# Thirty quarters of zeros: from fifteen plain writes on SyncE's queue to three casting writes on GpSimd's

## The chip, the core and the metric

The kernel runs on one core of a Trainium2 chip. The metric is the device time of one execution in microseconds (us). Each kernel is run several times and the median is given; one execution is also profiled.

The engines in play: TensorE (PE, matmuls; PEld is its weight load), VectorE (DVE), ScalarE (ACT), GpSimd (POOL), SyncE (SP, which here only issues DMAs), and 16 DMA engines which serve all queues. A queue is named by who issues into it; in the profile q1 is SyncE's, q10 ScalarE's, q0 GpSimd's, and q8 and q14 load instructions.

## What is computed

The inputs are `x` and `f_logit` (4 x 5056 x 256, four-byte floats), a gate vector, and the weights of eight experts (256 x 1024 and 1024 x 256 each). A recurrence runs along the 5056 steps of each of the 4 sequences, and each of the 20224 tokens that come out is sent to the expert with the largest logit. An expert keeps only the 80 tokens with the largest gate weight. All other rows of the output are zero.

```python
for t in range(S):
    h = f[:, t] * h + i[:, t] * x[:, t]      # f, i from a sigmoid of f_logit
    y[:, t] = h
# y as (20224, 256)
out = np.zeros((N, D), dtype=np.float32)
for e in range(E):
    tok_idx = np.where(expert_idx == e)[0]
    if len(tok_idx) > capacity:              # capacity = 80
        keep = np.argpartition(-gate_w[tok_idx], capacity)[:capacity]
        tok_idx = tok_idx[keep]
    h = np.maximum(x[tok_idx] @ w1[e], 0.0)
    out[tok_idx] = gate_w[tok_idx, None] * (h @ w2[e])
```

So 20.7 MB of zeros are written, and at most 640 rows of 1 KB are written over them.

## The kernel before

**Stage one, to about 120 us.** `f_logit` and `x` come in as 40 units (10 groups of 512 steps by 4 sequences; the last group is shorter), 512 KB each for either input. For each unit ScalarE makes the sigmoid, GpSimd the product, TensorE turns both to channels, VectorE runs the recurrence into `h_all`, TensorE makes the logits. SyncE issues all loads of this stage but one.

**Zeros.** The output is cut into 79 *quarters* of 256 rows (256 KB). The first four are written from a small zeroed tile (`first_zeros`). The list `zeros` holds the other 75 by number; two helpers take them from its front. `clear(k, m)` (L183) copies m quarters from the first four, so from output to output, with no buffer in SBUF. `wipe(m)` (L532 to L539) writes m pairs of quarters from `bare`, a weight buffer that ScalarE has filled with zeros (L530); 128 partitions of 4 KB make 512 KB, so a `wipe` of one is two quarters.

**Weights.** The experts' weights are 32 pieces of 512 KB, numbered here from 0 in the order in which TensorE uses them (`order`). They go round through a ring of 7 buffers that the first stage has set free (`ring`). `bare` lies in the last of them, which is the buffer of weight 6. A loop (L542) issues weights 0 to 6, with zeros after each: `m` counts of `wipe`, `k` quarters of `clear`. The tile framework puts in the waits: weight 6 is loaded only when every reader of `bare` is done with it, wherever in the program that reader stands. The other weights are issued by `more(1)` when TensorE has used up a buffer; the 11 quarters that are then left go between them.

**Order of work.** The schedule is written by hand (`tc.manual_schedule()`): each engine issues its instructions in the order of the program text, and an instruction that waits holds up those behind it on its own engine. SyncE issues every weight and every zero.

**Stage two, about 124 to 146 us.** The largest candidates are ranked. GpSimd fills `wide` with zeros (L666), then makes `level` (L667, L669) from `vals`, and `what` (L670, L678). VectorE makes `taken` from `level` (L687) and at last `trow`, the addresses of the chosen tokens. From about 146 us VectorE, ScalarE and GpSimd gather the chosen columns of `h_all` (L781), and from 149.7 us TensorE works through the experts: `hidden` (L817) with the first weights, `result` (L836, L846) with the second. The rows are scattered into the output (L873), after all zeros are in place.

Of the kernel before, what the change touches and what calls it, by code (L numbers as in the profile page):

```python
# [10 lines left out]
BF16 = mybir.dt.bfloat16  # L11
# [7 lines left out]
P = 128  # L19
# [16 lines left out]
def kernel(  # L36
# [11 lines left out]
    nc = tc.nc  # L48
    B, S, D = x.shape
    E, _, F = w1.shape  # L50
# [114 lines left out]
    ZR = 8  # L165
    ZC = 512
    ZQ = 4
    QP = P // ZQ
# [4 lines left out]
    zeros = list(range(ZQ, N // (QP * ZR)))  # L173
# [11 lines left out]
    def clear_some(m):  # L185
        while m > 0 and zeros:
            k = zeros[0]
            n = min(m, ZQ - k % ZQ, len(zeros))
            clear(k, n)
            del zeros[:n]  # L190
            m -= n
# [310 lines left out]
    for pool in ld[:-1]:  # L502
# [4 lines left out]
    order = sorted(((which, e, i) for which in (1, 2) for e in range(E) for i in range(2)),  # L507
                   key=e_step)
    order[-4], order[-3] = order[-3], order[-4]
    RING = 7  # L510
# [3 lines left out]
    def weights(which, e, i):  # L514
        t = ring[order.index((which, e, i)) % RING].tile([P, F], F32, name="w_sb", tag="w_sb")
        if which == 1:
            nc.sync.dma_start(out=t, in_=w1[e][ds(i * P, P)])
        else:
            t = t.rearrange("p (c d) -> p c d", c=CH)
            parts = 2 if (which, e, i) == order[-1] else 1  # L520
            n = CH // RUN // parts
            for k in range(parts):
                nc.sync.dma_start(
                    out=t.rearrange("p (h j) d -> p h j d", j=RUN)[:, ds(k * n, n)],
                    in_=w2[e][ds(i * FH + k * FH // parts, FH // parts)].rearrange(
                        "(h p j) d -> p h j d", p=P, j=RUN))
        return t

    bare = spare.tile([P, F], F32, name="w_sb", tag="w_sb")
    nc.scalar.activation(bare, ones.broadcast_to([P, F]), ACT.Copy, scale=0.0)  # L530
    BR = F // D

    def wipe(m):
        for _ in range(m):
            k = zeros[0]
            assert zeros[1] == k + 1 and 2 * QP * ZR == P * BR
            nc.sync.dma_start(out=out[ds(k * QP * ZR, P * BR)].rearrange("(p j) d -> p (j d)", p=P),
                              in_=bare)
            del zeros[:2]  # L539

    w_sb = {}
    for key, m, k in zip(order[:RING], (0, 0, 0, 0, 0, 15, 0), (0, 0, 2, 2, 1, 7, 7)):  # L542
        w_sb[key] = weights(*key)
        wipe(m)
        clear_some(k)
# [86 lines left out]
    with tc.tile_pool(name="sel", bufs=1) as sel:  # L632
# [27 lines left out]
        for k in range(BY_DVE, DEEP):  # L660
# [3 lines left out]
        what = sel.tile([P, DEEP, 2, E], F32, name="what")  # L664
        level = sel.tile([P, DEEP], F32, name="level")
        nc.gpsimd.memset(wide, 0.0)  # L666
        nc.gpsimd.tensor_scalar(out=level, in0=vals, scalar1=NONE, scalar2=-GONE,  # L667
                                op0=ALU.is_le, op1=ALU.mult)
        nc.gpsimd.tensor_tensor(level, level, bar, ALU.add)  # L669
# [281 lines left out]
    with tc.If(unsure > 0):  # L951
        with tc.tile_pool(name="all", bufs=1) as sel, \
# [34 lines left out]
            for g in range(NJ):  # L987
                nc.gpsimd.indirect_dma_start(
                    out=tok[:, ds(g, 1)], out_offset=None, in_=id_list,
# [46 lines left out]
```

## Time and profile before

| | us |
|---|---|
| median of 3 runs | 209.92 (209.12 to 211.46) |
| the profiled execution | 210.38 |
| its span in the profile | 208.6 |
| TensorE busy | 179.1 (86%) |
| VectorE busy | 152.1 (73%) |
| ScalarE busy | 137.7 (66%) |
| GpSimd busy | 131.5 (63%) |

80.10 MB pass through the 16 DMA engines at a mean of 384 GB/s. The span runs from the first to the last instruction of the profiled execution; 1.8 us of its time lie around it. Times in the rows below are counted from the span's start. The page cuts the span into 40 equal slices and gives for each the busy share of an engine in tenths (9 is 90% or more). A row of a wait names who waited, for whom, the total, how often, and the longest; the one named is the last that came.

### The profile page before, as it was taken

How to read it: one execution, taken by the hardware profiler on the slowest of the kernel's cores; microseconds unless marked ns; L12 is line 12 of the kernel's file. 1: busy time of each engine (PE TensorE's matmuls, PEld its weight loads, DVE VectorE, ACT ScalarE, POOL GpSimd, SP SyncE). 2: the span in 40 equal slices, each digit the busy share in tenths (PEclk: the TensorE clock that was granted, in tenths of full speed). 3: DMA queues.
4: the chain of work that ended last, by engine and by line, in shares of the span. 5: the costliest groups of instructions: out<-in, count | busy, mean ns of one | idle time of the engine just before them, and what ended most of it. 6: DMA issues, size and time to landing. Idle time of an engine off the chain costs nothing. (4 is left out here: it accounts for less than half of the span.)

```text
span 208.6 us, 7058 instructions
## 1 busy us (share of the span) xinstructions
PE 179.1 (86%) x2599; PEld 154.6 (74%) x2599; DVE 152.1 (73%) x485; ACT 137.7 (66%) x425; POOL 131.5 (63%) x245
## 2 busy tenths in 40 slices
PE   7779679999989999999989939798876899999880
PEld 7566568787878787887877817797875799987760
DVE  5587668999998989998999994894767637560020
ACT  2878498889887878787988952170994652771020
POOL 3385787989898878988697757100997540500621
PEclk9999999999999999999999976799999988999995
DMA  5999999999999999999999899999898999999941
GB/s 215 409 398 414 418 421 434 401 417 422 415 420 417 413 421 394 409 401 405 420 384 454 328 427 402 418 419 451 330 430 332 416 409 352 333 402 413 404 155 38
DMA packets 22541, 80.10 MB, mean 384 GB/s; under 512 B 2994, under 2 KB 2996, under 8 KB 21972
## 3 DMA queue, kind: packets, MB, share of 16 engines
q1 hardware_dynamic: 22112, 78.40, 94.3%
q0 software_dynamic: 240, 0.66, 0.9%
q8 instruction: 22, 0.36, 0.7%
q10 hardware_dynamic: 148, 0.53, 0.6%
q14 instruction: 19, 0.16, 0.2%
HBM read 70.00 MB, written 21.36 MB: 438 GB/s over the span
## 5 line engine op out<-in xcount | busy, mean ns | idle before, releaser
L278 POOL TENSOR_TENSOR x_t<-f_t,x_t 128x1024 f32<-128x1024 f32 (+1 forms) x39 | 91.2, 2346 | 16.5 <-DMA x_t<-in_x_dram 9.6
L327 DVE TENSOR_TENSOR_SCAN h_all<-h_all,up 128x512 f32<-128x512 f32 x72 | 86.1, 1254 | 5.8 <-ACT h_all L312 4.8
L312 ACT ACTIVATE h_all<-sp,nomlb 128x512 f32<-128x512 f32 x72 | 45.5, 682 | 10.0 <-PE sp L292 10.0
L274 ACT ACTIVATE f_t<-f_t 128x1024 f32<-128x1024 f32 (+1 forms) x40 | 42.1, 1053 | 10.6 <-DMA f_t<-in_f_logit_dram 9.7
L292 PE MATMUL up<-ident,x_t 128*128 128x128 f32 x288 | 38.0, 275 | 5.4 <-POOL x_t L278 5.2
L292 PE MATMUL sp<-ident,f_t 128*128 128x128 f32 x288 | 39.3, 279 | 0.7 <-ACT f_t L274 0.7
L292 PEld LDWEIGHTS up<-ident,x_t 128*128 128x128 f32 x288 | 31.9, 140 | 8.2 <-POOL x_t L278 7.8
L292 PEld LDWEIGHTS sp<-ident,f_t 128*128 128x128 f32 x288 | 30.9, 140 | 7.8 <-issue 5.2
L781 POOL COPY xe<-h_all 128x8 uint8 x160 | 22.2, 200 | 18.6 <-DVE xt L788 11.7
L339 PE MATMUL lg<-h_all,wg 128*32 128x128 f32 (+1 forms) x640 | 27.4, 286 | 6.3 <-ACT ls L348 4.0
L781 DVE COPY xe<-h_all 128x8 uint8 x256 | 20.5, 163 | 10.9 <-issue 10.8
L781 ACT COPY xe<-h_all 128x8 uint8 x224 | 22.7, 194 | 4.4 <-issue 2.8
L339 PEld LDWEIGHTS lg<-h_all,wg 128*32 128x32 f32 x640 | 15.4, 109 | 13.7 <-ACT ls L348 6.1
L817 PE MATMUL h_ps<-xt,w_sb 128*64 128x80 f32 x512 | 22.1, 240 | 2.9 <-DVE xt L788 1.9
L817 PEld LDWEIGHTS h_ps<-xt,w_sb 128*64 128x64 f32 x512 | 19.8, 142 | 4.0 <-DVE xt L788 2.1
L836 PE MATMUL y_ps<-hid,w_sb 128*64 128x80 f32 x448 | 19.2, 238 | 3.8 <-issue 1.7
L836 PEld LDWEIGHTS y_ps<-hid,w_sb 128*64 128x64 f32 x448 | 17.2, 140 | 5.5 <-issue 4.0
L197 PE MATMUL warm<-ident 128*128 128x128 f32 x128 | 19.4, 321 | 1.4 <-POOL ident masks.py:199 1.4
L197 PEld LDWEIGHTS warm<-ident 128*128 128x128 f32 x128 | 18.7, 234 | 1.6 <-POOL ident masks.py:199 1.4
L873 POOL DMA_INDIRECT out_dram<-y,goal x5 | 5.1, 1022 | 18.9 <-DMA w_sb<-in_moe_w_dram 14.2
L826 ACT ACTIVATE hid<-h_ps 128x320 f32<-128x320 f32 x16 | 6.5, 432 | 9.0 <-PE h_ps L817 8.9
L870 DVE TENSOR_SCALAR y<-y_ps,gsl 128x256 f32<-128x256 f32 x4 | 1.9, 480 | 12.9 <-DMA out_dram<-y,goal 11.1
(142 smaller groups left out, 143.9 us busy)
## 6 DMA issues: line engine op xcount, KB each, us to landing
f_t<-in_f_logit_dram SPq DMA_DIRECT2D x36, 512.0 KB, 6.3
x_t<-in_x_dram SPq DMA_DIRECT2D x35, 512.0 KB, 6.7
w_sb<-in_moe_w_dram SPq DMA_DIRECT2D x31, 512.0 KB, 8.3
out_dram<-w_sb SPq DMA_DIRECT2D x15, 512.0 KB, 10.0
out_dram<-out_dram SPq DMA_DIRECT2D x27, 256.0 KB, 7.5
f_t<-in_f_logit_dram SPq DMA_DIRECT2D x4, 448.0 KB, 5.1
x_t<-in_x_dram SPq DMA_DIRECT2D x4, 448.0 KB, 5.8
out_dram<-out_dram SPq DMA_DIRECT2D x2, 768.0 KB, 8.4
```

The costliest lines, as they stand in the source:

```text
L197: nc.tensor.matmul(warm, ident, ident, start=True, stop=True)
L274: nc.scalar.activation(s_t, s_t, ACT.Sigmoid, scale=-1.0)
L278: (nc.gpsimd if n else nc.vector).tensor_tensor(u_t, sts[n], u_t, ALU.mult)
L292: nc.tensor.transpose(at, t[:, ds(r * D + o * P, P)], ident)
L312: nc.scalar.activation(columns(n, o).rearrange("c (p r) -> c p r", r=R), sps.pop((n, o)).rearrange("c (r p) -> c p r", r=R), ACT.Identity, ...
L327: nc.vector.tensor_tensor_scan(h, h, ups.pop((n, o)), last, ALU.mult, ALU.add)
L339: nc.tensor.matmul(lgs[g][ds(r * LC, LC), b, :k], wg[:, o], h[:, r], start=o == 0, stop=o == DC - 1, skip_group_check=True)
L781: copy(xe[:, :, ds(WORD * (k + j), WORD)], pair(v - HOME))
L817: nc.tensor.matmul(HP[e, i][ds(j, HC), c], w[1, e, o][:, at:at + (HC - 1) * RUN + 1:RUN], XT[e][:, o], start=o == 0 and c == 0, stop=o == ...
L826: nc.scalar.activation(HID[e, i], HP.pop((e, i)), ACT.Relu)
L836: nc.tensor.matmul(YP[e][ds(j, HC), o], w[2, e, i][:, c, ds(o * P + j, HC)], HID[e, i][:, c], start=i == 0 and c == 0 and o == 0, stop=i = ...
L873: one = nc.gpsimd.indirect_dma_start(out=out, out_offset=bass.IndirectOffsetOnAxis(ap=goal[:, ds(g, 1)], axis=0), in_=Y.pop(g), in_offset= ...
```

## The change

SyncE's fifteen `wipe` writes are dropped (the count 15 becomes 0). In their place a new helper, `widen(n, m)`, issues n transfers on GpSimd's queue, each of m blocks of 512 KB, taken from the front of `zeros`; `widen(3, 5)` is three transfers of 2.5 MB (as written), 30 quarters in all. It reads `bare` as two-byte floats, 1024 of them in each partition, m times over, and writes four-byte floats, 20 KB in one piece for each partition. The call stands in GpSimd's program behind the fill of `wide` and ahead of `level`. The `clear` counts stay, so the numbers of the quarters that each helper takes shift; 11 quarters are left for the spread between the later weights, as before.

```diff
+    def widen(n, m):
+        k = zeros[0]
+        assert zeros[2 * n * m - 1] == k + 2 * n * m - 1 and 2 * QP * ZR == P * BR
+        small = bare.bitcast(BF16)[:, :F].unsqueeze(1).broadcast_to([P, m, F])
+        for _ in range(n):
+            nc.gpsimd.dma_start(
+                out=out[ds(zeros[0] * QP * ZR, m * P * BR)].rearrange(
+                    "(p m j) d -> p m (j d)", p=P, m=m), in_=small)
+            del zeros[:2 * m]
+
     w_sb = {}
-    for key, m, k in zip(order[:RING], (0, 0, 0, 0, 0, 15, 0), (0, 0, 2, 2, 1, 7, 7)):
+    for key, m, k in zip(order[:RING], (0, 0, 0, 0, 0, 0, 0), (0, 0, 2, 2, 1, 7, 7)):
         w_sb[key] = weights(*key)
         wipe(m)
         clear_some(k)
...
         nc.gpsimd.memset(wide, 0.0)
+        widen(3, 5)
         nc.gpsimd.tensor_scalar(out=level, in0=vals, scalar1=NONE, scalar2=-GONE,
                                 op0=ALU.is_le, op1=ALU.mult)
```

## Rows read from the trace of the kernel before

**Rows 1.** The page's head, and the busy shares in 40 slices (tenths).

```profile
span 208.6 us, 7058 instructions
PE 179.1 (86%) x2599; PEld 154.6 (74%) x2599; DVE 152.1 (73%) x485; ACT 137.7 (66%) x425; POOL 131.5 (63%) x245
...
DMA  5999999999999999999999899999898999999941
```

**Rows 2.** The DMA queues: packets, MB, share of 16 engines' span.

```profile
q1 hardware_dynamic: 22112, 78.40, 94.3%
q0 software_dynamic: 240, 0.66, 0.9%
q8 instruction: 22, 0.36, 0.7%
```

**Rows 3.** Stretches: us, then each engine's busy time, PEclk, DMA share, GB/s.

```profile
30.00:100.00 70.00, 67.16 (x834) 56.92 (x833) 65.56 (x76) 58.89 (x82) 61.32 (x31) 1.00 1.02 413
130.00:146.00 16.00, 13.62 (x110) 13.10 (x110) 11.69 (x41) 5.62 (x23) 1.23 (x5) 0.89 1.05 429
146.00:150.00 4.00, 3.41 (x35) 3.22 (x35) 3.02 (x36) 4.00 (x42) 3.92 (x28) 1.00 0.96 396
150.00:152.00 2.00, 2.00 (x64) 2.00 (x60) 1.60 (x22) 2.00 (x22) 2.00 (x15) 1.00 0.61 168
...
173.00:183.00 10.00, 10.00 (x268) 9.62 (x266) 6.54 (x73) 5.76 (x43) 2.74 (x20) 0.98 0.97 341
```

**Rows 4.** Timeline of SyncE's queue: start, us, issue, count.

```profile
121.05 0.39 SPq L523 DMA_DIRECT2D w_sb<-in_moe_w_dram  x1
122.52 15.62 SPq L537 DMA_DIRECT2D out_dram<-w_sb  x15
139.05 3.00 SPq L183 DMA_DIRECT2D out_dram<-out_dram  x3
149.50 0.35 SPq L517 DMA_DIRECT2D w_sb<-in_moe_w_dram  x1
...
151.11 0.56 SPq L523 DMA_DIRECT2D w_sb<-in_moe_w_dram  x1
```

**Rows 5.** Waits of SyncE's queue, 120 to 152 us: total, times, longest.

```profile
SPq L517 <- DMA out_dram<-w_sb: 7.3, 1, 7.3
```

**Rows 6.** Timeline of TensorE: start, us, group, count, idle before it and its releaser.

```profile
159.83 0.36 PE L836 MATMUL y_ps<-hid,w_sb 128*64 128x80 f32 x4 [1.71 <-issue]
...
161.94 1.33 PE L836 MATMUL y_ps<-hid,w_sb 128*64 128x80 f32 x32 [0.65 <-DMA w_sb<-in_moe_w_dram]
...
165.18 1.52 PE L836 MATMUL y_ps<-hid,w_sb 128*64 128x80 f32 x32 [0.75 <-DMA w_sb<-in_moe_w_dram]
```

**Rows 7.** Waits of TensorE from 149 to 206 us.

```profile
PE y_ps L836 <- issue: 1.7, 1, 1.7
PE y_ps L836 <- DMA w_sb<-in_moe_w_dram: 1.4, 2, 0.8
PE h_ps L817 <- DMA w_sb<-in_moe_w_dram: 0.6, 1, 0.6
PE y_ps L836 <- SPq L951: 0.5, 1, 0.5
```

**Rows 8.** Timeline of GpSimd, and of VectorE's first use of `level`.

```profile
129.70 0.34 POOL L666 MEMSET wide<- 16x304 f32 x1
134.79 0.32 POOL L667 TENSOR_SCALAR level<-vals 128x12 f32<-128x12 f32 x1 [4.75 <-ACT last_of L640]
...
140.93 0.17 DVE L687 SCALAR_TENSOR_TENSOR taken<-rank,level 128x12 f32<-128x12 f32 x1
```

**Rows 9.** GpSimd's scatter: duration in ns, and us from issue to landing.

```profile
L873 POOL DMA_INDIRECT out_dram<-y,goal x5: 974/976/1202, 194.2 to 203.1; - x5
...
DMA to landing us min/median/max: 2.4/4.5/5.7
```

**Rows 10.** DMA issues of the weights: count, KB each, median us to landing.

```profile
w_sb<-in_moe_w_dram SPq DMA_DIRECT2D x31, 512.0 KB, 8.3
```

## The prediction

> **What bounds the kernel now.** I read first the head of the page, its slices and its queues. The 16 DMA engines stand at nine tenths or more in nearly every slice up to the last two, while the busiest compute engine, TensorE, has 86% [rows 1]. Almost all of that is one queue, SyncE's: 78.40 MB in 94.3% of the engines' time [rows 2]. The table by stretches then says what a byte costs. From 30 to 100 us the core only loads (HBM to SBUF) and takes back a few output-to-output copies: 413 GB/s at a share of 1.02, that is 405 at a share of one. From 130 to 146 us the 15 writes out of the zeroed buffer run (SBUF to HBM): 429 at 1.05, that is 409. From 146 to 150 us come mostly copies from output to output, which touch no SBUF: 396 at 0.96, that is 412 [rows 3]. (A packet counts where it starts, so a share can pass 1.) On each route a byte costs the same: the engine is what is full, not a side of it. One stretch of 2 us has a hole: 0.61 of the engines at 150 to 152 us. Another, 173 to 183 us, runs at 341 GB/s, where weights are asked for only as TensorE frees their buffers.
>
> Then SyncE's own order. It issues weight 5 at 121.05, the 15 zero writes from 122.52 to 138.14, seven quarters of copies at 139.05, and weight 6 at 149.50 [rows 4]. The 7.3 us ahead of weight 6 are a wait for the last zero write [rows 5]: weight 6 goes into the buffer that the zeros are read from. The seven copies, issued before that wait, feed the engines meanwhile, so the wait costs only the hole. Last, TensorE: it first runs short of weights at 161.94 (weight 7, issued at 151.11) [rows 4, 6]. After 149 us its waits for weights make 1.4 + 0.6 us, and 0.5 us more go to the queue that asks for one [rows 7]. So TensorE and the transfers are almost level from 160 us to the end, and whatever delays weight 7 delays the end; whatever speeds the transfers up wins little more than those 2.5 us.
>
> **The change part by part.** *Removed from SyncE:* 15 issues. They pace SyncE, but the engines are full behind them, so the removal by itself is worth nothing.
>
> *Added to GpSimd:* three transfers behind the fill of `wide`, which ends at 129.70 + 0.34 = 130.04 [rows 8]. Each has 128 x 5 rows of 4 KB written and 2 KB read. GpSimd makes their descriptors itself. Before shows that only for the scatter, 976 ns for 128 rows [rows 9]. Bounds for one transfer of 640 rows: 1.0 us (as one scatter) to 5 x 0.976 = 4.9 us. Three take 3 to 14.6 us. GpSimd's next work needs `vals` and runs at 134.79; VectorE takes `level` at 140.93 [rows 8]. GpSimd has about 1.2 us of its own to do in between, so the cover is 140.93 - 130.04 - 1.2 = 9.7 us. I take 2 us each, 6 in all (a plain pattern, nearer to the one scatter's fixed cost than to five of them), which is hidden. At the upper bound the ranking would come 14.6 - 9.7 = 4.9 us late.
>
> *Same bytes written:* 15 x 524,288 = 7.86 MB, at 420 GB/s 18.7 us of all engines. What a casting transfer costs, no row shows, since before every transfer reads as much as it writes. Bounds: half (only the read bytes count), 9.4 us; the dearest queue per byte, q8, whose 0.36 MB took 0.7% of the engines where q1 pays 94.3 / 78.40 = 1.20% for a MB, is 1.94 / 1.20 = 1.6 times as dear, 30 us [rows 2]. GpSimd's own queue, q0, pays 0.9 / 0.66 = 1.36%, 1.13 times, 21.2 us [rows 2]. I take 1.0 for the casting writes: q0's row is of five small scatters with their ends counted, and the engine must still put out 4 KB for each row.
>
> *Moved without a line in the diff:* the order around weight 6. It still waits for the zeros to be read, but the seven copies that followed the zeros now go ahead of them. SyncE issues them right behind weight 5 and then stops at weight 6 with the next seven copies, weight 7 and all later ones queued behind. Seven quarters are 1.84 MB, 4.4 us at 420 GB/s. In front of the zeros instead of behind, they put off the end of the zeros and so weight 6: 149.50 + 4.4 = 153.9 us (**+4.4**).
>
> *The way back:* in before weight 7 reached TensorE 161.94 - 149.50 = 12.4 us after weight 6 was issued, partly behind the rest of the seven copies. In after the engines stand empty then. Two weights and seven quarters are 2.88 MB, 7.0 us at 413 GB/s; to this comes the latency, between 2.1 us (the quickest scatter landed after 2.4 us [rows 9], of which its 128 KB are 0.3) and twice that. So 9.1 to 11.2 us, against 12.4: -1.2 to -3.3, I take **-2.2**.
>
> *A hole ahead of the zeros:* weight 5 lands about 8.3 us after its issue [rows 10], near 129.4, and the seven copies end some 4.4 us later less the latency, near 132. GpSimd starts at 130.04. With 1 us of descriptors and 1 us of latency there is no hole; with 4.9 there are about 3.3 us more than the copies cover. I take **+1.0**.
>
> Sum: 4.4 - 2.2 + 1.0 = **+3.2 us** for weight 7, hence for TensorE at 161.94. From there on it runs with next to no wait for weights up to 191 us, so it carries the delay to the end. Bounds: 4.4 - 3.3 + 0 = +1.1, and 4.4 - 1.2 + 3.3 = +6.5.
>
> The profiled execution took 210.38 us (span 208.6 and 1.8 around it), 0.46 above the median of 209.92. It would become 213.6; against the median, 213.1.
>
> **Rivals.** *A cheap cast (faster).* If an engine's time follows the bytes it reads, the zeros take 9.4 us, weight 6 is issued near 144.5, weight 7 at 151.11 without a queue, and both arrive before they are needed. The gain ends where TensorE is level: its waits of 2.5 us, at most with the 1.7 us of its own issue stall [rows 7] as instruction loads find free engines. That gives 209.92 - 2.5 = 207.4, down to 205.7; break-even is where the zeros cost (18.7 - 3.2) / 18.7 = 0.83 of a plain write. For it speaks only that half the bytes are read; against it that the three routes of [rows 3], with and without SBUF, cost the same, as if the engine's own path set the pace and 4 KB must still leave it. The Trainium skill (DMA: Bandwidth & Descriptors, "Where 436 GB/s comes from") names the 16 ports into SBUF, 32 bytes each at 850 MHz, as the bottleneck; by that rule two-byte reads would halve the zeros, to about 9 us as an estimate from that page. The trace does not agree as far as it goes: the copies that use no SBUF port ran at the same 412 GB/s.
>
> *A dear cast.* At q8's 1.6 the zeros take 11.3 us more and nothing else is in the queues, so weight 6 waits it all out: 213.1 + 11.3 = 224.4. At q0's 1.13 it is 215.5. For it: the conversion is work that no plain transfer has.
>
> *A late GpSimd.* At the upper bound of its descriptors the ranking comes 4.9 us late, and with it the gather. TensorE has 1.7 + 0.65 us of waits [rows 6] before 161.94 to absorb it, so 2.5 us remain, in the shadow of weight 7's +3.2; with the hole at 3.3 also due then, the end is at +6.5 at most: 216.4.
>
> *A wash.* A cast at 0.75 to 0.93 of a write, or the order costing only its lower bound, +1.1: 208.5 to 212.0. Here too belongs that the transfers run on a queue of their own and change only who issues. The Trainium skill (DMA: Bandwidth & Descriptors, "Issuing engines are not separate DMA queues") says that DMAs from all three issuers share the same 16 engines, and by that alone nothing would be won or lost.
>
> **How the numbers follow.** My forecast, plain cost and the order's delay, with the late GpSimd in it: 0.50, own range 211.0 to 216.4, some 0.07 of it within 1%. Dear cast from 1.25 times up: 0.15, from 217.5. Cheap cast: 0.25, of which 0.02 stays within 1%. Wash: 0.10. A measurement of this kernel tells about 1%, 2.1 us, from no change. So faster 0.23, same 0.19, slower 0.58. The range from 206.0 to 218.5 leaves out the lower end of the cheap case (some 0.07) and most of the dear one (0.12).
>
> **What would show it.** In after: weight 6 issued near 154 and TensorE waiting for weights around 160 to 165 us, with a hole in the DMA share before 155 us, shows the order's delay. The share of q0 against its 8.5 MB gives the price of a cast: 1.2% per MB is plain, 0.6 cheap. GpSimd's three issues and the start of `level` show the cover. I am wrong if q0's share is near half, if weight 6 goes out before 149 us, or if the first gather starts late.

## The result, and the profile after

| | before, us | after, us |
|---|---|---|
| median of 19 runs each | 211.46 (209.12 to 213.81) | 212.99 (211.39 to 216.26) |
| the profiled execution | 210.38 | 211.39 |
| its span | 208.6 | 209.6 |

The ratio of after to before is 1.0105, with a 95% interval of 1.0072 to 1.0137. Of 211.46 us that is 2.2 us more (1.5 to 2.9). So the kernel became about 1% slower. (The ratio leaves out the executions in the chip's slower state, so it is not that of the two medians, which lie 1.5 us apart.) Single executions of either kernel scatter by 4 to 5 us, so the pair of profiles (1.0 us apart) can show the mechanism but not its size.

The page's head, its DMA slices in tenths, and the queues (packets, MB, share of the 16 engines' span) of after:

```profile
span 209.6 us, 7048 instructions
...
DMA  6999999999999999999999999999795999999941
...
q1 hardware_dynamic: 19952, 70.53, 84.1%
q0 software_dynamic: 2208, 8.52, 12.1%
```

7.86 MB moved from SyncE's queue to GpSimd's, and two slices fall to 7 and 5 tenths where [rows 1] has 8 and 8. The timeline of SyncE's queue (start, us, issue) shows what happened at its left edge, and the wait row of the same queue (total, times, longest) names the cause:

```profile
119.61 0.39 SPq L523 DMA_DIRECT2D w_sb<-in_moe_w_dram  x1
120.79 1.16 SPq L183 DMA_DIRECT2D out_dram<-out_dram  x2
152.42 0.33 SPq L517 DMA_DIRECT2D w_sb<-in_moe_w_dram  x1
152.79 1.77 SPq L183 DMA_DIRECT2D out_dram<-out_dram  x3
154.66 0.53 SPq L523 DMA_DIRECT2D w_sb<-in_moe_w_dram  x1
...
SPq L517 <- DMA out_dram<-w_sb: 30.3, 1, 30.3
```

Weight 5 at 119.61, the seven copies right behind it, and then SyncE stands for 30.3 us until the zeros have been read out of weight 6's buffer. In before it stood 7.3 us at the same place, with the zeros and the seven copies issued in between [rows 4, 5]. Weight 7 goes out at 154.66, against 151.11.

The stretches show that the transfers ran dry while SyncE stood. The columns are those of [rows 3]; the last three are PEclk, DMA share and GB/s. First before:

```profile
131.00:149.00 18.00, 16.47 (x135) 16.06 (x135) 13.23 (x69) 7.84 (x51) 4.11 (x25) 0.91 1.06 435
149.00:153.00 4.00, 2.59 (x66) 2.28 (x64) 3.02 (x34) 4.00 (x42) 4.00 (x29) 1.00 1.03 369
```

The same stretches of after, and the next:

```profile
131.00:149.00 18.00, 15.51 (x146) 14.78 (x147) 13.36 (x73) 8.99 (x62) 6.14 (x35) 1.00 1.23 415
149.00:153.00 4.00, 2.86 (x84) 2.70 (x81) 2.62 (x31) 4.00 (x43) 4.00 (x30) 1.00 0.27 85
153.00:157.00 4.00, 3.93 (x114) 3.77 (x110) 2.92 (x33) 4.00 (x34) 3.76 (x28) 1.00 1.41 461
```

From 149 to 153 us only 85 GB/s move. At 415 that stretch would have carried (415 - 85) x 4 = 1.32 MB more, which is 3.2 us of transfers lost. Before had its hole here too [rows 3], but a small one. (A packet counts where it starts, and the copies' packets are long, so the 461 behind the hole is partly work that runs on after 157.)

TensorE then pays for it. Its timeline in after (start, us, group, count, idle before it and releaser), its longest waits from 149 to 206 us, and one stretch of 1 us:

```profile
156.95 1.28 PE L828 MATMUL h_ps<-xt,w_sb 128*64 128x80 f32 x32
163.73 2.40 PE L847 MATMUL y_ps<-hid,w_sb 128*64 128x80 f32 x32 [5.51 <-DMA w_sb<-in_moe_w_dram]
165.89 1.59 PE L828 MATMUL h_ps<-xt,w_sb 128*64 128x80 f32 x32
...
203.42 0.60 PE L952 MATMUL h_ps<-ident,yc 128*128 128x128 f32 x2
...
PE y_ps L847 <- DMA w_sb<-in_moe_w_dram: 5.5, 1, 5.5
PE h_ps L828 <- DVE xt L799: 1.1, 1, 1.1
...
164.00:165.00 1.00, 1.00 (x20) 1.00 (x19) 0.86 (x12) 0.00 (x0) 0.00 (x0) 0.50 0.88 340
```

It waits 5.51 us for weight 7, where before waited 0.65 [rows 6], and starts on it at 163.73 instead of 161.94. After the idle time the granted clock is 0.50 from 164 to 165 us, the lower of the two levels (1.2 GHz), and 32 matmuls take 2.40 us instead of 1.33 [rows 6]. Behind that nothing waits long for a weight again, and the last group ends at 204.02: the delay is carried to the end.

GpSimd's side, from its timeline and from the view of the line that issues the zeros (duration in ns, first and last start; then us to landing):

```profile
129.17 2.69 POOL L546 DMA_DIRECT2D out_dram<-w_sb  x3
133.99 0.30 POOL L678 TENSOR_SCALAR level<-vals 128x12 f32<-128x12 f32 x1 [2.12 <-ACT last_of L650]
...
L546 POOL DMA_DIRECT2D out_dram<-w_sb x3: 910/920/1088, 129.2 to 130.8; - x3
...
DMA to landing us min/median/max: 10.8/16.0/21.5
```

Each issue takes 0.9 us, the three are over at 131.86, and GpSimd then idles 2.12 us for ScalarE, as it idled 4.75 us before [rows 8]. The last transfer lands 21.5 us after its issue at 130.8, that is at 152.3, just ahead of weight 6.

### The profile page after: what moved, and what is told of

It is laid out like the page before. It is cut to its first block, busy times and chain, and to the rows that moved or that the text cites. A ratio compares the mean times of both kernels' runs of the same rounds, so it can differ in the third digit from the quotient of the medians.

```text
span 209.6 us, 7048 instructions
## 1 busy us (share of the span) xinstructions
PE 176.5 (84%) x2599; PEld 152.9 (73%) x2599; DVE 150.6 (72%) x485; ACT 137.9 (66%) x425; POOL 134.0 (64%) x248
## 3 DMA queue, kind: packets, MB, share of 16 engines
q0 software_dynamic: 2208, 8.52, 12.1%
## 5 line engine op out<-in xcount | busy, mean ns | idle before, releaser
L847 PE MATMUL y_ps<-hid,w_sb 128*64 128x80 f32 x448 | 19.7, 242 | 7.0 <-DMA w_sb<-in_moe_w_dram 5.5
L828 PE MATMUL h_ps<-xt,w_sb 128*64 128x80 f32 x512 | 21.6, 236 | 2.8 <-DVE xt L799 1.6
L847 PEld LDWEIGHTS y_ps<-hid,w_sb 128*64 128x64 f32 x448 | 17.7, 143 | 8.3 <-issue 8.0
L197 PE MATMUL warm<-ident 128*128 128x128 f32 x128 | 17.9, 304 | 1.4 <-POOL ident masks.py:199 1.4
L197 PEld LDWEIGHTS warm<-ident 128*128 128x128 f32 x128 | 17.3, 218 | 1.6 <-POOL ident masks.py:199 1.4
L881 DVE TENSOR_SCALAR y<-y_ps,gsl 128x256 f32<-128x256 f32 x4 | 1.9, 479 | 13.0 <-DMA out_dram<-y,goal 11.3
```

The lines of the kernel that those rows point to most:

```text
L197: nc.tensor.matmul(warm, ident, ident, start=True, stop=True)
L828: nc.tensor.matmul(HP[e, i][ds(j, HC), c], w[1, e, o][:, at:at + (HC - 1) * RUN + 1:RUN], XT[e][:, o], start=o == 0 and c == 0, stop=o == ...
L847: nc.tensor.matmul(YP[e][ds(j, HC), o], w[2, e, i][:, c, ds(o * P + j, HC)], HID[e, i][:, c], start=i == 0 and c == 0 and o == 0, stop=i = ...
```

## The experiments

Two theories went in. **Order:** the loss comes from seven copies standing ahead of the zeros instead of behind them, which leaves the engines empty while SyncE waits for weight 6's buffer. **Price:** the loss comes from the casting transfers being dearer than plain ones. Each ratio below is to the kernel before, measured on the same chip.

| run | ratio | 95% interval |
|---|---|---|
| after, twice more (e8_after, e9_after) | 1.0110, 1.0102 | 1.0055 to 1.0166, 1.0055 to 1.0149 |
| e1_plain, again as e9_plain | 1.0190, 1.0128 | 1.0105 to 1.0274, 1.0038 to 1.0219 |
| e2_order | 1.0060 | 1.0002 to 1.0117 |
| e5_both, again as e9_both | 0.9997, 1.0023 | 0.9951 to 1.0043, 0.9971 to 1.0076 |
| e4_behind | 1.0228 | 1.0152 to 1.0305 |
| e3_own | 1.0388 | 1.0313 to 1.0463 |
| e6_pad | 1.0015 | 0.9963 to 1.0067 |
| e7_more | 1.0044 | 0.9996 to 1.0092 |
| e9_both_plain | 1.0136 | 1.0054 to 1.0218 |

**The same transfers without the cast.** After, with four-byte zeros read:

```diff
-        small = bare.bitcast(BF16)[:, :F].unsqueeze(1).broadcast_to([P, m, F])
+        small = bare.unsqueeze(1).broadcast_to([P, m, F])
```

> The three transfers stay on GpSimd's queue and in their place, but read four-byte zeros, so nothing is cast. Theory of the order (the loss comes from weight 6 being issued later, with empty engines behind the zeros, and a cast costs what a plain write costs): as the changed kernel, +1.5 to +2.5 us over the kernel before, weight 6 near 152 to 154 us, the hole behind the zeros still there. Theory of the price (the cast is dearer: GpSimd's queue paid 12.1% for 8.52 MB, 1.42% a MB, against 84.1 / 70.53 = 1.19 on SyncE's, so 1.19 times, 3.6 us on 18.7): back at the time of before or within 0.5 us of it, weight 6 some 3 us earlier, and 1.2% a MB.

Queue, stretch, and weight 6's issue of this kernel; then, from 135 to 147 us, when next to nothing but the zeros is under way, the rows of after, of this kernel and of e2_order (below, plain zeros on SyncE's queue):

```profile
q0 software_dynamic: 2208, 8.52, 10.2%
...
131.00:149.00 18.00, 16.45 (x135) 15.88 (x134) 11.46 (x51) 6.26 (x35) 3.43 (x16) 0.91 1.01 404
...
151.71 0.33 SPq L517 DMA_DIRECT2D w_sb<-in_moe_w_dram  x1
...
135.00:147.00 12.00, 10.91 (x104) 10.53 (x103) 8.41 (x50) 6.55 (x40) 2.44 (x16) 1.00 1.25 424
135.00:147.00 12.00, 11.16 (x105) 10.78 (x104) 6.62 (x27) 4.30 (x17) 0.35 (x1) 1.00 1.03 420
135.00:147.00 12.00, 11.09 (x104) 10.71 (x104) 7.75 (x41) 5.25 (x27) 1.33 (x9) 1.00 1.03 416
```

Without the cast GpSimd's queue takes 10.2 / 8.52 = 1.20% of the engines per MB, with it 12.1 / 8.52 = 1.42%. Yet the stretch moves 404 GB/s without and 415 with it, and in the 12 us of zeros alone the rates are level: 424 with the cast, 420 without it, 416 without it on SyncE's queue. The cast's packets last longer and overlap more (the share is 1.03 here, 1.25 in after), but the throughput is that of plain ones, and weight 6 goes out only 0.7 us earlier. The total is not lower than after's. Price falls.

**The order alone, on SyncE, without the cast.** Before, with the copies ahead of the wipes:

```diff
         w_sb[key] = weights(*key)
-        wipe(m)
         clear_some(k)
+        wipe(m)
```

> The kernel before with one pair of lines swapped: the seven quarters of copies are issued ahead of the fifteen plain zero writes instead of behind them. No cast, nothing on GpSimd. Theory of the order: slower than before by 1.5 to 3 us, weight 6 issued near 153 to 154 us, a hole in the DMA share behind the last zero, TensorE's long wait for weight 7. Theory of the price, and a theory that GpSimd's issues are what costs: no difference from before, within 0.5 us.

```profile
120.03 0.38 SPq L523 DMA_DIRECT2D w_sb<-in_moe_w_dram  x1
152.12 0.34 SPq L517 DMA_DIRECT2D w_sb<-in_moe_w_dram  x1
...
149.00:153.00 4.00, 2.44 (x64) 2.28 (x64) 3.17 (x37) 3.94 (x40) 4.00 (x30) 1.00 0.26 101
...
164.69 2.31 PE L836 MATMUL y_ps<-hid,w_sb 128*64 128x80 f32 x32 [4.94 <-DMA w_sb<-in_moe_w_dram]
```

The whole signature of after is here with nothing on GpSimd and nothing cast: weight 6 at 152.12, 101 GB/s in the same 4 us, 4.94 us of waiting for weight 7, and the slow 32 matmuls behind it. So two swapped lines make the mechanism. The ratio, 1.0060, is 1.3 us (0.0 to 2.5), a little under the 1.5 to 3 expected and somewhat below after's; the intervals overlap. Part of the difference shows in the profiles: from weight 5's issue to weight 6's it is 152.12 - 120.03 = 32.09 us here and 32.81 in after. That fits with after's engines running short once more, ahead of the zeros. From 129 to 134 us, after and then e2_order:

```profile
129.00:134.00 5.00, 2.91 (x23) 2.51 (x22) 4.04 (x13) 1.28 (x5) 2.87 (x5) 1.00 0.88 284
129.00:134.00 5.00, 3.43 (x17) 3.20 (x17) 3.92 (x12) 1.25 (x5) 0.29 (x2) 0.67 0.85 350
```

That is (350 - 284) x 5 = 0.33 MB, or 0.8 us of transfers. Whether the rest of the difference is more than scatter stays open.

**Bridging the hole.** After, with seven copies given to GpSimd's queue behind the zeros. In the first kernel those are the seven that stood ahead of the zeros, in the second the seven that stand between weights 6 and 7:

```diff
-    for key, m, k in zip(order[:RING], (0, 0, 0, 0, 0, 0, 0), (0, 0, 2, 2, 1, 7, 7)):
+    for key, m, k in zip(order[:RING], (0, 0, 0, 0, 0, 0, 0), (0, 0, 2, 2, 1, 0, 7)):   # e4_behind
+    for key, m, k in zip(order[:RING], (0, 0, 0, 0, 0, 0, 0), (0, 0, 2, 2, 1, 7, 0)):   # e5_both
...
         widen(3, 5)
+        clear_some(7, nc.gpsimd)
```

> The changed kernel with the first seven quarters of copies moved from SyncE's queue to GpSimd's, behind the three casting transfers, so that they again run while weight 6 waits for the zeros, as in before. Theory of the order: the loss is gone, within 1 us of before, weight 6 near 149 to 150 us, the hole behind the zeros about as small as before; some of it may stay if the engines run empty at 128 to 131 us, since the copies no longer bridge the time until GpSimd issues (up to +3 us). Theory of the price: 3 us or more slower than before.

> The changed kernel with the second seven quarters of copies moved from SyncE's queue, where they stand behind weight 6, to GpSimd's, behind the three casting transfers. The first seven stay ahead, on SyncE's queue. So copies bridge both places where the engines ran empty: 127 to 131 us, before GpSimd's first zeros, and 149 to 153 us, while weight 6 waits for the last of them. Theory of the order (all of the loss is engines standing idle): the engines stay full, and the loss of 1% is gone: -0.5 to +0.5% against before, weight 7 about 3 us sooner behind weight 6. Theory of the price (a cast on GpSimd's queue costs more than a plain write): still about 1% slower, with no hole left to blame.

The first, e4_behind:

```profile
127.00:131.00 4.00, 2.76 (x12) 1.84 (x10) 2.74 (x9) 1.22 (x4) 3.92 (x9) 0.50 0.07 28
...
165.00 2.40 PE L848 MATMUL y_ps<-hid,w_sb 128*64 128x80 f32 x32 [5.91 <-DMA w_sb<-in_moe_w_dram]
```

It was expected to lose the loss, or to keep up to 3 us of it if the engines ran empty ahead of the zeros; it was slower still, by 4.8 us (3.2 to 6.5), which is not all accounted for. The seven copies had covered the time until GpSimd's zeros flow; without them 127 to 131 us run at 28 GB/s. The zeros end only 0.8 us earlier for that (weight 6 at 151.65), and weight 7 again has seven copies ahead of it. The hole moved; it did not close.

The second, e5_both, and its repetition's PE row:

```profile
149.00:153.00 4.00, 2.85 (x84) 2.69 (x80) 2.72 (x32) 4.00 (x42) 4.00 (x30) 1.00 1.26 497
...
159.68 1.93 PE L829 MATMUL h_ps<-xt,w_sb 128*64 128x80 f32 x32 [2.46 <-DMA w_sb<-in_moe_w_dram]
```

```profile
158.92 1.33 PE L829 MATMUL h_ps<-xt,w_sb 128*64 128x80 f32 x32 [1.54 <-DMA w_sb<-in_moe_w_dram]
```

> The third corner: the changed kernel with the second seven quarters of copies on GpSimd's queue behind the zeros. Theory of the order: as the kernel before, within 0.5%.

Here weight 6 goes out no earlier than in after (153.34), but the hole carries the seven copies, and weight 7 follows weight 6 directly. TensorE waits 2.46 us (1.54 in the repetition) for weight 6 and next to nothing for weight 7. The loss is gone, twice: 0.9997 and 1.0023. As this kernel keeps the cast and GpSimd's issues, those two cost nothing that can be measured.

**Weight 6 free of the zeros.** After, with the zeros read from a small tile of their own, 2 KB a row in e3_own (in a pool beside the others) and 512 bytes a row in e6_pad (in constants that the kernel holds anyway, so rows of 1 KB are written):

```diff
-        small = bare.bitcast(BF16)[:, :F].unsqueeze(1).broadcast_to([P, m, F])
+        small = nil.bitcast(BF16).unsqueeze(1).broadcast_to([P, m, F])              # e3_own
+        small = nil.bitcast(BF16).unsqueeze(1).broadcast_to([P, 4 * m, 2 * PAD])    # e6_pad
```

> The changed kernel, but the two-byte zeros are read from a 2 KB tile of their own that GpSimd fills at 130 us, so weight 6 no longer waits for the zeros. Casts, queue and place are as in the changed kernel. Theory of the order: the loss is gone, and as weights 6 and 7 no longer stand behind the zeros TensorE's waits of 1.4 us at 162 and 165 us go too: 0 to 2.5 us faster than before, weight 6 issued near 124 us, no hole at 150. Theory of the price: the zeros still take 3.6 us more of all engines, so still 1.5 us or more slower than before.

> The changed kernel, but the two-byte zeros are read from a 512-byte tile of their own that no later tile reuses (256 of them a row, 1 KB written a row, four times as many rows), so weight 6 waits for no zeros and no expert tile does either. Casts, queue and place as in the changed kernel. Theory of the order: weight 6 issued near 123 us, no hole near 150, and weights 6 and 7 no longer behind the zeros: 0 to 1.2% faster than before. Theory of the price: still about 1% slower. Either way, should GpSimd take over 9.7 us for the descriptors of 7680 rows (640 took 0.92 us), its ranking work and the first gather come late, by up to 2 us.

```profile
122.74 0.50 SPq L517 DMA_DIRECT2D w_sb<-in_moe_w_dram  x1
...
158.79 5.09 PE L830 MATMUL h_ps<-xt,w_sb 128*64 128x80 f32 x96 [10.32 <-DVE xt L801]
...
  DMA out_dram<-nil: 10.2, 1
...
122.42 0.98 SPq L517 DMA_DIRECT2D w_sb<-in_moe_w_dram  x1
```

In e3_own (the first three rows; the third is VectorE's wait before it writes `xt`) weight 6 goes out at 122.74 as meant, but the new tile's memory is used again by the experts' input `xt`, so the gather waits for the zeros instead and the first matmul starts at 158.79. The 3.9% are that new wait's, an artefact of the edit. e6_pad (the last row: weight 6 at 122.42) has no such neighbour: its loss is gone (1.0015), but it gains nothing measurable over before, where 0 to 1.2% was expected.

**All fourteen copies ahead of weight 6, in before.** It asks whether before's own small hole is worth closing:

```diff
-    for key, m, k in zip(order[:RING], (0, 0, 0, 0, 0, 15, 0), (0, 0, 2, 2, 1, 7, 7)):
+    for key, m, k in zip(order[:RING], (0, 0, 0, 0, 0, 15, 0), (0, 0, 2, 2, 1, 14, 0)):
```

> The kernel before with all fourteen quarters of copies between the zeros and weight 6, where before has seven ahead of weight 6 and seven behind it. No cast, nothing on GpSimd. Theory of the order: weight 6 is still issued near 149.5 us, but 8.7 us of copies then cover its wait, so before's own hole of 0.6 us at 150 to 152 us closes, and weight 7 comes right behind weight 6: 0 to 1 us faster than before. A rival (the hole in before costs nothing, since TensorE is level there): no difference.

```profile
147.67 0.35 SPq L517 DMA_DIRECT2D w_sb<-in_moe_w_dram  x1
...
160.66 1.70 PE L817 MATMUL h_ps<-xt,w_sb 128*64 128x80 f32 x32 [3.16 <-DMA w_sb<-in_moe_w_dram]
```

A miss: 0 to 1 us faster was expected, 0.9 us slower came (-0.1 to 1.9), which the rival, no difference, would also allow. Fourteen copies ahead of weight 6 keep the engines full, but it has to queue behind them, and TensorE waits 3.16 us for it.

**The square: hole or bridge, cast or plain.** That e1_plain was not faster asked for one more look. After and e1_plain were run again together with e5_both (as e9_after, e9_plain and e9_both) and with e5_both without the cast (e9_both_plain). After had been repeated once before, beside e5_both, e6_pad and e7_more (e8_after).

```diff
-        small = bare.bitcast(BF16)[:, :F].unsqueeze(1).broadcast_to([P, m, F])
+        small = bare.unsqueeze(1).broadcast_to([P, m, F])
```

> The changed kernel itself once more, unaltered, on the chip of the three below, to compare them with it. Theory of the order and theory of the price alike: 0.7 to 1.4% slower than before, weight 6 near 152 us, engines idle from about 149 to 153 us.

> The changed kernel, unaltered, as one corner of a square of four on one chip: casting or plain reads, with copies behind the zeros or without. Theory of the order: 0.6 to 1.6% slower than before, as both times until now.

> The second corner: as the changed kernel, but the zeros are read as four-byte floats, so nothing is cast. Theory of the order (the cast neither costs nor saves): within 0.5% of the changed kernel in the same call. A new theory, from the first trial of this edit (1.9% slower, and its first loads of token addresses took 3.8 us instead of 1.1 to 1.3): four-byte reads of SBUF hold those loads up, the cast spares them, so 0.7 to 1% slower than the changed kernel and the long loads again.

> The fourth corner: as the third, with four-byte reads and no cast. Theory of the order: as the third and as the kernel before, within 0.5%. The new theory of the four-byte reads: 0.7 to 1% slower than the third, with first loads of token addresses near 3.8 us.

| | hole left | hole bridged |
|---|---|---|
| two bytes read (cast) | 1.0102 | 1.0023 |
| four bytes read (plain) | 1.0128 | 1.0136 |

Bridging takes the loss away only with the cast. The profile shows where the plain kernel loses instead. GpSimd's loads of the token addresses into registers, ahead of the gather (min/median/max in ns, first and last start), in after, e9_both, e1_plain, e9_plain, e9_both_plain and e2_order in turn, then in before and e7_more:

```profile
L776 POOLq TENSOR_LOAD <-trow x16: 321/690/1300, 143.3 to 179.8; - x16
L777 POOLq TENSOR_LOAD <-trow x16: 319/689/1291, 143.6 to 177.0; - x16
L776 POOLq TENSOR_LOAD <-trow x16: 319/1024/3788, 143.5 to 179.5; - x16
L776 POOLq TENSOR_LOAD <-trow x16: 319/1012/3728, 143.5 to 181.2; - x16
L777 POOLq TENSOR_LOAD <-trow x16: 318/825/2342, 143.4 to 179.7; - x16
L765 POOLq TENSOR_LOAD <-trow x16: 318/752/2329, 143.5 to 181.1; - x16
L765 POOLq TENSOR_LOAD <-trow x16: 321/688/1452, 144.3 to 177.9; - x16
L765 POOLq TENSOR_LOAD <-trow x16: 317/691/1290, 143.4 to 178.4; - x16
```

And TensorE's wait for the gathered input in e1_plain and in e9_both_plain:

```profile
PE h_ps L828 <- DVE xt L799: 4.0, 1, 4.0
...
PE h_ps L829 <- DVE xt L800: 3.3, 1, 3.3
```

The slowest load takes 1.3 us in the two kernels that cast and 2.3 to 3.8 us in the next four, which do not, with the zeros on GpSimd's queue or on SyncE's (e2_order). In the three of them on GpSimd's queue TensorE then waits 3.3 to 4.0 us for the first input; after's longest such wait is 1.1. With the hole left, that wait hides in the one for weights (2.2 us in e1_plain, 5.5 in after); with the hole bridged nothing hides it. The two intervals of the bridged column in this comparison still overlap a little (1.0054 to 1.0218, 0.9971 to 1.0076), that of e5_both lies clear (up to 1.0043).

That the loads are held up by the plain reads themselves is not shown, and the last two rows speak against it in so simple a form. Before and e7_more read four-byte zeros too, and the last of these had not landed when their loads began at 144.3 and 143.4 us, since weight 6, which waits for it, goes out at 149.50 and 147.67. Yet their slowest loads took 1.45 and 1.29 us. In the four slow kernels weight 6 goes out later, at 151.71 to 154.06. So slow loads were seen only beside plain reads, but not beside all of them, and what makes the difference stays open.

## Why the prediction was right, and where it was off

The forecast was 213.1 us, 3.2 above a median of 209.92; measured are a median of 212.99 and, by the ratio, 2.2 us (1.5 to 2.9) more than before, whose median more runs put at 211.46. Direction, mechanism and range held; the size was 1.0 us too large, and nearly equal absolute times are owed to the base that rose by 1.5.

- *The order, +4.4: right, with 3.6 of its own.* Counted from weight 5's issue, weight 6 goes out after 152.42 - 119.61 = 32.81 us, against 149.50 - 121.05 = 28.45 [rows 4]: +4.36. (Weight 5 is issued ahead of all that the change touches; the 1.44 us by which the profiled executions differ there are scatter.) e2_order, which has the order alone, takes 32.09: +3.64. It shows the cause by itself, and e5_both that the loss is gone without the hole.
- *The hole ahead of the zeros, +1.0: there, about 0.7.* That is what is left of the +4.36 (0.6 in e9_after), and the 0.8 us of transfers that after lacks from 129 to 134 us agree. The size was right, the descriptors were not: 0.9 us each were needed where 2 were taken. In after's own times the prediction's working gives, as an estimate, 129.17 + 0.9 + 1 us against copies that end near 119.61 + 10.95 = 130.6, so 0.5. (Its upper bound is a slip: with 4.9 us the same working gives 130.04 + 4.9 + 1 - 132 = 3.9 us, not 3.3, and 7.1 for the sum.) e4_behind shows what the first seven copies cover.
- *The way back, -2.2: too large by half.* Weight 7 reached TensorE 163.73 - 152.42 = 11.3 us after weight 6's issue, against 12.4: -1.1, just outside the bounds of -1.2 to -3.3. The estimate let weight 7 be asked for at once; SyncE issued weight 6 and three groups of copies first, so that weight 7 went out 154.66 - 152.42 = 2.2 us later. The first two terms came out 1.0 us too large together and this one 1.1 us too large the other way, and that they cancel is luck: from weight 5 to TensorE's start on weight 7 it is 44.12 us against 40.89, +3.23, with a forecast of +3.2.
- *From there to the end: carried, as said.* From 163.73 to 204.02 are 40.3 us; 161.94 to 202.42 in before are 40.5. A term that the sum lacked, the lower clock behind a long wait (2.40 instead of 1.33 us for the first 32 matmuls), cost 1.1 us, and was mostly taken up by a wait that before has in the same place (0.75 us at 165.18 [rows 6]). One pair of profiles thus gives +3.0 to +3.2, the ratio of all runs +2.2; the rest is not explained beyond the scatter of single executions.
- *The cast at a plain price: right, by a wrong yardstick.* "1.2% per MB is plain" would have read 1.42% as dear. The share did rise, the throughput did not fall: 424 GB/s against 420 from 135 to 147 us. A cheap cast is out too: halved reads did not halve the time. The Trainium skill (DMA: Bandwidth & Descriptors, "Where 436 GB/s comes from") calls the ports into SBUF the bottleneck, though it adds that between HBM and SBUF the HBM side binds. The trace does not show the ports to set the pace on this route: halving what is read there bought 1%.
- *GpSimd hidden: right, and easier than thought.* 2.69 us in all where 6 was taken. Nor did the gather start late: TensorE's first expert matmul comes at 148.60 us, against 149.74 in before.
- *The wash, by which the transfers "change only who issues": wrong here,* since the issue order at a waiting queue decides what the engines have to do meanwhile.

No theory of the prediction had that the cast would help anything. With the zeros in the changed place, TensorE's first expert matmul comes at 148.60 us in after and 152.31 in e1_plain, at 148.83 in e9_both and 151.49 in e9_both_plain. That fits with the cast version, bridged, standing level with before and the plain one not. It is no gain over plain zeros as before issues them: e7_more, which has them on SyncE's queue ahead of the copies, starts at 148.68. No version that ran is measurably faster than before: the best, e5_both, equals it.

## What to carry to other kernels

Moving transfers from one queue to another moves everything that stood around them, even with no line of it in the diff: write down for the waiting queue what is issued ahead of its wait and whether that covers the wait. Close such a hole with work that stood *behind* the late transfer, on another queue (e5_both): the work ahead of it covers something already (e4_behind), and on the same queue the late transfer has to wait behind it (e7_more). And judge a transfer's price by the GB/s of a stretch in which it is alone, since a queue's share of the engines can rise without costing anything.

## What was not expected of the hardware

From 135 to 147 us, transfers from two-byte zeros to four-byte ones ran at 424 GB/s written, plain ones from the same place at 420, while the share of the engines per MB was 1.42% against 1.20%. GpSimd made the descriptors of 640 rows in 0.92 us, where the scatter takes 0.976 us for 128 [rows 9] and e6_pad's transfers 1.41 us for 2560: four times the rows cost half as much again.

The loads of addresses into GpSimd's registers took up to 1.3 us in the kernels that cast. In those that do not it was up to 3.8 us where the zeros ended late (e1_plain) and 1.3 where they ended early (e7_more), and TensorE's first expert matmul came up to 3.7 us later with the slow loads. The Trainium skill (DMA: Bandwidth & Descriptors, "Latency and other measured facts") gives about 600 ns as the floor of such a load; the rows here go from 317 ns, below that floor, to 3788.
